# Twelve products that nothing reads, put in front of the two products of the first token unit for which TensorE waits last

## The chip, the cores and the metric

The kernel runs on one core of a Trainium2 chip. The metric is the device time of one execution in microseconds, the median of three runs. Times inside an execution come from one execution that the hardware profiler recorded; they count from the start of its span. The engines are TensorE (PE, with its weight loads PEld), VectorE (DVE), ScalarE (ACT), GpSimd (POOL) and SyncE (SP), which issues the transfers.

## What is computed

A windowed attention is followed by a gated mixing of tokens and channels. The reference, cut to what matters:

```python
# attention: q, k, v are (8, 8, 576, 64); heads 0-3 see the 32 positions up to their own,
# heads 4-7 every fourth of 128
scores = scale * np.matmul(q, k.transpose(0, 1, 3, 2))
scores = np.where(masks[None, :, :, :], scores, -1000000000.0)
scores = scores - np.max(scores, axis=-1, keepdims=True)
attn = np.exp(scores)
attn = attn / (np.sum(attn, axis=-1, keepdims=True) + 1e-09)
attn_out = np.matmul(attn, v)
# x is (8, 576, 512): the heads side by side
theta = x @ w_theta
zr = x * np.cos(theta)
zi = x * np.sin(theta)
y = einsum('ts,bsd->btd', w_tok_r, zr) + einsum('ts,bsd->btd', w_tok_i, zi)
u = x + y
return u + np.maximum(u @ w_ch, 0.0)
```

## The kernel before

The work goes batch by batch (8 batches). The attention of a batch is done in four pairs of heads: `scores` (products on TensorE into a bank of the pool s, line 468), row maxima and exponentials, `turn` (transposes on VectorE, line 525) and `pv` (products with v into the bank of tag v, line 617). For some pairs the mask is added by TensorE itself, with products of the identity (line 424) that open the score bank; then VectorE takes the row maxima from the bank (line 430) and scales them (line 438), and ScalarE reads the bank with its exponentials (line 485), five for the first part of a pair and four for the second. The bank is free when the last of them has read it. The pool s has two banks.

`theta` and `trig` make theta, sines and cosines, and `zsplit` splits each block kt of z into a rounded part zh (ScalarE, line 644, or VectorE, line 641) and the rest zl (GpSimd, line 646). There are nine blocks: 0 to 3 are x times the cosine and 4 to 7 x times the sine in four blocks of 128 tokens, and 8 holds the last 64 tokens of both.

A token unit, `token(b, d, g)`, makes one 128x288 piece of y: 128 channels d by half g of the tokens. For each block kt, in the order KORD = (0, 4, 1, 5, 2, 6, 3, 7, 8), it issues three products: zh with the upper part of the token weights (wtkh), zh with the lower part (wtkl), and zl with the upper part; 27 products in all, into one bank. `residual` then adds the bank to x on VectorE (line 825), and ScalarE and GpSimd split the sum (lines 828 and 830). Channel units, `chan`, follow in the same way (line 882). A batch has 16 units: four token units of g = 0, four of g = 1, and eight channel units. In batch 0 the units take turns on the two banks of the pool m, so that the fourth unit needs the bank whose sums the residual of the second has read.

The order on each engine is fixed ahead of time by the class `Order`, a planner with costs and ranks, for batch 0 and the beginning of batch 1, and by program order after that. In batch 0 TensorE's row is kept as the planner wrote it: the products of the first token unit stand between the last work on theta and the scores of batch 1, and each waits for its block of z. The last blocks to come are zh and zl of block 3. The second and third token unit follow directly; the scores of pairs 2 and 3 of batch 1 stand between the products of the third and fourth, and the outputs of pair 0 of batch 1 (line 617) within the fourth.

Of the kernel before, what the change touches and what calls it, by code (L numbers as in the profile page):

```python
# [10 lines left out]
BF16 = mybir.dt.bfloat16  # L11
# [7 lines left out]
DM = H * D  # L19
# [19 lines left out]
FG0 = {4: ("zl2", "zl6"), 0: ("zl3", "zl7"), 1: ("zh3", "zh7")}  # L39
COS_PSUM, SIN_PSUM = True, True  # L40
KORD = (0, 4, 1, 5, 2, 6, 3, 7, 8)
TP0 = {4: "s", 0: "s", 1: "x", 2: "t", 3: "s"}
TP = {4: "t", 0: "s", 1: "s", 2: "t", 3: "s"}

# [17 lines left out]
class Order:  # L62
# [17 lines left out]
    def signal(self, event):  # L80
        self.events[event] = self.now

    def go(self, gen, rank=None):
        if not self.live:
            for _ in gen:
                pass
            return
        self.serial += 1
        t = [self.rank if rank is None else rank, self.serial, self.now, gen, None, 0.0]
        self.tasks.append(t)  # L90
        self.advance(t)
# [60 lines left out]
def build(ctx, tc, qT, kT, vw, wth, wtk, wch, maskb, ident, identb, outT):  # L152
    nc = tc.nc
    cp = ctx.enter_context(tc.tile_pool(name="const", bufs=1))
# [15 lines left out]
    def pe(ins):  # L170
        tc.keep_in_program_order(ins)
# [13 lines left out]
    def reserve(tag):  # L185
        taken[tag] = taken.get(tag, -1) + 1
        return taken[tag]

    def take(tag, bufs, n=None):
        n = reserve(tag) if n is None else n  # L190
        if od.live:
            if n >= bufs:
                yield None, ("free", tag, n - bufs)
            if n:
                yield None, ("got", tag, n - 1)
            signal(("got", tag, n))
        return n

    def give(tag, n):
        if od.live:  # L200
            signal(("free", tag, n))

    def bank(tag, name):
        if tag == "v":
            n = yield from take(tag, 1)
            return ps_v.tile([128, 2 * DM], F32, tag=tag, name=name), (tag, n)
        pl, bufs = banks[tag]
        n = yield from take(tag, bufs)
        return pl.tile([128, DM], F32, tag=tag, name=name), (tag, n)
# [60 lines left out]
    def first_loads():  # L270
        yield "DMA", dma(3 * BW + 64)
        pin(nc.sync.dma_start(mskb, maskb.bitcast(BF16)))
        pin(nc.sync.dma_start(idb, identb.bitcast(BF16)))
        for pr in range(NP):
            yield from take(f"xh{pr}", 1, 0)
            yield from take(f"u{pr}", 1, 0)
            pqs.append(hp.tile([128, 2, S], F32R, tag=f"xh{pr}", name=f"P0_{pr}").bitcast(F32)[:, 0])
            q = hp.tile([128, 2, S], F32R, tag=f"u{pr}", name=f"q0_{pr}").bitcast(F32)
            q = q.rearrange("p a b -> p (a b)").rearrange("p (a b) -> p a b", b=2 * QB)
            k = first_k[:, KE * pr:KE * pr + KE]  # L280
            yield "DMA", dma(2 * S)
            pin(nc.sync.dma_start(q, qT[0, pr]))
            yield "DMA", dma(KE)
            pin(nc.sync.dma_start(k, kT[0, pr]))
            qks[0, pr] = (q, k, None)
            if pr == 0:
                yield "DMA", dma(128)
                pin(nc.sync.dma_start(idt, ident))
            signal(("qk", 0, pr))
        for pr in range(NP // 2):  # L290
            v = first_v[:, NJ * 128 * pr:NJ * 128 * pr + NJ * 128].rearrange("p (a b) -> p a b", b=128)
            yield "DMA", dma(NJ * 128)
            pin(nc.sync.dma_start(v, vw[0, pr]))
            for h, t in (("a", v[:, :VA]), ("b", v[:, VA:])):
                vs[h, 0, pr] = (t, None)
                signal(("v" + h, 0, pr))
        for pr in range(NP // 2, NP):
            yield from load_va(pr)
            yield from load_vb(pr)
# [354 lines left out]
    def theta0(st):  # L654
        cs = slice(128 * st, min(128 * st + 128, S))
        n = cs.stop - cs.start
        for c in range(NC):
            yield None, ("wth32", c)
            yield None, ("xe", 0, c)
            if c == 0:  # L660
                if TP0[st] == "s":
                    yield None, ("sc", 0, NP - 1)
                elif TP0[st] in "tm":
                    yield None, ("fl", 0, NP - 1)
                ths[0, st] = yield from bank(TP0[st], f"th0_{st}")
            yield "PE", 860
# [150 lines left out]
    def residual(b, d, g, ps, rel):  # L817
        ts = slice(HS * g, HS * g + HS)
        x = xf[b, d]
        if g == 0:  # L820
            yield from take(f"u{d}", 1, UH.get(d) if b == 0 else None)
            u = hp.tile([128, 2, S], F32R, tag=f"u{d}", name=f"u{b}_{d}")
            uh[b, d], ul[b, d] = u[:, 0], u[:, 1]
        yield "DVE", dve(HS)
        pin(nc.vector.tensor_tensor(x[:, ts], ps, x[:, ts], op=ALU.add))  # L825
        give(*rel)
        yield "ACT", act(HS)
        pin(nc.scalar.copy(uh[b, d][:, ts], x[:, ts]))  # L828
        yield "POOL", pool(HS)
        pin(nc.gpsimd.tensor_tensor(ul[b, d][:, ts], x[:, ts], uh[b, d][:, ts].bitcast(F32), op=ALU.subtract))  # L830
        signal(("u", b, d, g))

    def unit_bank(b, n):
        return "mmx"[n % 3] if b else "m"

    def token(b, d, g):
        yield None, ("z", b, KORD[0])
        yield None, ("wtk", g, KORD[0] // 2)
        ps, rel = yield from bank(unit_bank(b, NC * g + d), f"y{b}_{d}_{g}")
        ps = ps[:, :HS]  # L840
        cs = slice(128 * d, 128 * d + 128)
        n = 0
        for kt in KORD:
            yield None, ("z", b, kt)
            yield None, ("wtk", g, kt // 2)
            zh, zl = zs[b, kt]
            wh, wl = (w[:, HS * (kt % 2):HS * (kt % 2) + HS] for w in wtks[g, kt // 2])
            yield "PE", 369
            for l, r in ((zh, wh), (zh, wl), (zl, wh)):
                pe(nc.tensor.matmul(ps, l[:, cs], r, start=(n == 0), stop=(n == 3 * NK - 1)))  # L850
                n += 1
        signal(("tk", b, d, g))
        go(residual(b, d, g, ps, rel), RANK["evacuate"])

# [14 lines left out]
    def chan(b, e, g):  # L869
# [14 lines left out]
        go(finish(b, e, g, ps, rel), RANK["evacuate"])  # L884

    UNITS = [(token, d, g) for g in range(2) for d in range(NC)]
    UNITS += [(chan, e, g) for g in range(2) for e in range(NC)]

# [64 lines left out]
    EA, LA, LA2 = ([(t, reserve(t)) for t in ts] for ts in (EARLY, LATE, LATE2))  # L953
    XH = {p: reserve(f"xh{p}") for p in range(NP)}
    UH = {d: reserve(f"u{d}") for d in range(NC)}
    od.live = True
    go(first_loads(), 0)
    go(consts(), 0)
# [100 lines left out]
```

## Time and profile before

| | |
|---|---|
| median of 3 runs | 584.02 us (583.85 to 584.76) |
| the profiled execution | 585.12 us |
| its span | 583.3 us |
| mean granted TensorE clock | 0.987 |
| TensorE busy | 553.4 us (95%), 5464 products |
| VectorE busy | 377.9 us (65%) |
| ScalarE busy | 343.9 us (59%) |
| GpSimd busy | 222.5 us (38%) |

TensorE is busy for nearly the whole span. Its granted clock is at one of two levels, 2.4 GHz (full, 1.00 in the rows) and 1.2 GHz (half, 0.50). In a profile a product's duration contains its way through the array, so what a product costs in a row of products is read from the distance between two starts. Idle time in front of an instruction stands in brackets with the engine, the tile and the line that ended it.

### The profile page before, as it was taken

What the parts mean: (1) busy time and instruction counts of PE and PEld (TensorE: products, weight loads), DVE (VectorE), ACT (ScalarE), POOL (GpSimd) and SP (SyncE); (2) the same over time, 40 slices, a digit from 0 to 9 for tenths busy, and PEclk for the clock granted to TensorE, in tenths of its full rate; (3) what the DMA queues carried; (4) which work ended last, traced back from release to release, by engine and by line L of the source; (5) the groups of instructions that cost most, each with busy time, mean ns of one, the idle gap of its engine ahead of it and who ended that gap; (6) DMA issues with size and microseconds to landing.
All of it is one profiled execution on the core that took longest, in us unless ns stands there. A gap on an engine that the chain in (4) does not pass through costs nothing.

```text
span 583.3 us, 13997 instructions
## 1 busy us (share of the span) xinstructions
PE 553.4 (95%) x5464; PEld 503.5 (86%) x5464; DVE 377.9 (65%) x1156; ACT 343.9 (59%) x939; POOL 222.5 (38%) x206
## 2 busy tenths in 40 slices
PE   5997799999999899999999899998999899999997
PEld 3744698879999799988999799988999799989997
DVE  3779798866666768666765767666775667545112
ACT  1498967767554784459555695349645685267110
POOL 2227855525124362326324263225423262326120
PEclk9999699899999999999999999999999999999999
DMA  8990437601748056460746246470746323331002
GB/s 300 400 360 16 172 101 247 212 0 75 215 144 200 25 175 211 100 174 27 261 144 162 65 144 202 116 197 1 251 146 165 96 83 102 66 98 60 24 0 82
DMA packets 45586, 81.91 MB, mean 140 GB/s; under 512 B 3920, under 2 KB 19024, under 8 KB 45520
## 3 DMA queue, kind: packets, MB, share of 16 engines
q1 hardware_dynamic: 45520, 81.02, 43.9%
q8 instruction: 43, 0.70, 0.5%
q14 instruction: 23, 0.19, 0.1%
HBM read 64.49 MB, written 16.52 MB: 139 GB/s over the span
## 4 chain that ended last, share of the span: by engine, by line
DVE 31%; PE 29%; ACT 26%; POOL 6%; issue 4%; DMA 3%; SPq 1%; ACTq 0%; DVEq 0%
DVE pt L525 14%; PE y L850 13%; ACT P L504 10%; PE c L882 7%; PE th L685 4%; DVE P L409 4%; POOL zl L646 3%; DVE xh L599 2%; POOL P L510 2%; ACT zh L644 2%; ACT K L698 2%; ACT K L787 2%; PE s L468 2%; ACT cos L705 2%; ACT th L796 2%
## 5 line engine op out<-in xcount | busy, mean ns | idle before, releaser
L830 POOL TENSOR_TENSOR u<-x,u 128x288 fp32r<-128x288 f32 x64 | 54.9, 858 | 190.1 <-ACT u L828 190.1
L525 DVE STREAM_TRANSPOSE pt<-P 32x288 f32<-32x288 f32 x224 | 105.1, 469 | 12.1 <-POOL P L510 8.5
L882 PE MATMUL c<-u,late_wc 128*128 128x288 f32 x768 | 108.9, 295 | 0.0
L882 PEld LDWEIGHTS c<-u,late_wc 128*128 128x128 f32 x768 | 105.9, 188 | 2.8
L850 PE MATMUL y<-wtkh,zh 128*128 128x288 f32 x288 | 90.4, 314 | 1.8 <-ACT zh L644 1.8
L828 ACT CAST u<-x 128x288 fp32r<-128x288 f32 x64 | 27.4, 429 | 108.0 <-DVE x L825 108.0
L850 PE MATMUL y<-wtkh,zl 128*128 128x288 f32 x288 | 86.4, 300 | 4.0 <-POOL zl L646 4.0
L646 POOL TENSOR_TENSOR zl<-g,zh 128x512 fp32r<-128x512 f32 x40 | 52.6, 1317 | 94.8 <-ACT zh L644 81.9
L850 PE MATMUL y<-wtkl,zh 128*128 128x288 f32 x288 | 86.0, 299 | 0.0
L685 PE MATMUL th<-wthh,xh 128*128 128x512 f32 x224 | 75.1, 396 | 7.4 <-DVE g L748 7.4
L504 ACT ACTIVATE P<-P,mx 128x64 f32<-128x64 f32 x216 | 72.0, 335 | 10.3 <-DVE mx L498 9.6
L850 PE MATMUL y<-late_wt_b,zh 128*128 128x288 f32 x320 | 68.2, 297 | 0.0
L825 DVE TENSOR_TENSOR x<-y,x 128x288 f32<-128x288 f32 x64 | 28.6, 450 | 54.9 <-PE y L850 54.6
L850 PEld LDWEIGHTS y<-wtkh,zh 128*128 128x128 f32 x288 | 55.3, 192 | 5.3 <-ACT zh L644 2.9
L850 PEld LDWEIGHTS y<-wtkh,zl 128*128 128x128 f32 x288 | 55.3, 192 | 4.7 <-POOL zl L646 4.7
L685 PEld LDWEIGHTS th<-wthh,xh 128*128 128x128 f32 x224 | 42.0, 187 | 17.3 <-issue 8.4
L850 PE MATMUL y<-late_wt_a,zh 128*128 128x288 f32 x256 | 56.8, 304 | 0.0
L850 PEld LDWEIGHTS y<-wtkl,zh 128*128 128x128 f32 x288 | 55.3, 192 | 0.3 <-issue 0.3
L510 POOL TENSOR_TENSOR P<-P,sm 128x576 f32<-128x576 f32 x32 | 37.5, 1172 | 42.0 <-DVE sm L508 18.1
L850 PEld LDWEIGHTS y<-late_wt_b,zh 128*128 128x128 f32 x320 | 51.5, 189 | 0.3
L850 PE MATMUL y<-late_wt_b,zl 128*128 128x288 f32 x160 | 47.3, 296 | 0.0
L581 ACT COPY x<-o 128x576 f32<-128x576 f32 x32 | 29.7, 928 | 28.8 <-PE o L617 24.0
(108 smaller groups left out, 1107.6 us busy)
## 6 DMA issues: line engine op xcount, KB each, us to landing
q<-in_qT_dram SPq DMA_DIRECT2D x32, 576.0 KB, 5.1
va<-in_vw_dram SPq DMA_DIRECT2D x30, 320.0 KB, 3.4
k<-in_kT_dram SPq DMA_DIRECT2D x28, 304.0 KB, 5.7
out_dram<-x SPq DMA_DIRECT2D x28, 288.0 KB, 2.3
vb<-in_vw_dram SPq DMA_DIRECT2D x29, 256.0 KB, 3.8
xd<-xq SPq DMA_DIRECT2D x24, 288.0 KB, 5.2
xn<-xd SPq DMA_DIRECT2D x24, 256.0 KB, 5.1
st_wtk<-in_wtk_dram SPq DMA_DIRECT2D x8, 576.0 KB, 9.1
```

The source lines that it names most:

```text
L409: pin(nc.vector.tensor_tensor_reduce(out=P[:, n], in0=ps[:, n - g0], in1=mskb[:, mask_of(pr, n)], op0=ALU.add, op1=ALU.max, scale=1.0, sca ...
L504: table(nc.scalar.activation(P[:, n], P[:, n], AF.Exp, bias=mx[:, n:n + 1], scale=SCALE, accum_out=sm[:, n:n + 1]))
L510: pin(nc.gpsimd.tensor_tensor(P, P, sm.unsqueeze(2).to_broadcast([128, NJ, BW]), op=ALU.mult))
L525: pin(nc.vector.transpose(pmats[b, pr][k0:k0 + QB, :, hh, QB * e:QB * e + QB], P[p0:p0 + QB, :, QB * o:QB * o + QB]))
L581: pin(nc.scalar.copy(dst, src))
L646: pin(nc.gpsimd.tensor_tensor(lo, z, hi.bitcast(F32), op=ALU.subtract))
L685: pe(nc.tensor.matmul(pt, l, r, start=(n == 0), stop=(n == 3 * NC - 1)))
L825: pin(nc.vector.tensor_tensor(x[:, ts], ps, x[:, ts], op=ALU.add))
L828: pin(nc.scalar.copy(uh[b, d][:, ts], x[:, ts]))
L830: pin(nc.gpsimd.tensor_tensor(ul[b, d][:, ts], x[:, ts], uh[b, d][:, ts].bitcast(F32), op=ALU.subtract))
L850: pe(nc.tensor.matmul(ps, l[:, cs], r, start=(n == 0), stop=(n == 3 * NK - 1)))
L882: pe(nc.tensor.matmul(ps, l[:, cs], r[:, ts], start=(n == 0), stop=(n == 3 * NC - 1)))
```

## The change

Twelve products of a tile of ones with itself are put into the first token unit (batch 0, d = 0, g = 0): eight in front of the first product of block 3, and four in front of its third product. They are bf16, 128 by 512, write the bank of tag v, and nothing reads that bank before it is written anew. The bank is taken from the planner ahead of block 3 and given back at the end of the unit. The tile of ones is filled once, by VectorE, at the start of the program.

```diff
+KEEP_BUSY = {(0, 0, 0, 3, 0): 8, (0, 0, 0, 3, 2): 4}
...
             zh, zl = zs[b, kt]
             wh, wl = (w[:, HS * (kt % 2):HS * (kt % 2) + HS] for w in wtks[g, kt // 2])
+            if (b, d, g, kt) == (0, 0, 0, KORD[6]):
+                busy = yield from bank("v", "busy")
             yield "PE", 369
-            for l, r in ((zh, wh), (zh, wl), (zl, wh)):
+            for i, (l, r) in enumerate(((zh, wh), (zh, wl), (zl, wh))):
+                for _ in range(KEEP_BUSY.get((b, d, g, kt, i), 0)):
+                    pe(nc.tensor.matmul(busy[0][:, :DM], ones[:, :128], ones, start=True, stop=True))
                 pe(nc.tensor.matmul(ps, l[:, cs], r, start=(n == 0), stop=(n == 3 * NK - 1)))
                 n += 1
+        if b == d == g == 0:
+            give(*busy[1])
         signal(("tk", b, d, g))
...
+    ones = cp.tile([128, DM], BF16, name="ones")
+    nc.vector.memset(ones, 1.0)
     od.live = True
```

TensorE's row before, at the end of block 6 and in block 3 of the first unit (y_0_0 is the unit's bank; the last number of a name is a running one):

```order
L850 MATMUL y_0_0_648<-wtkl_623,zh_6_692 128x288
L850 MATMUL y_0_0_648<-wtkh_622,zl_6_693 128x288
L850 MATMUL y_0_0_648<-wtkh_526,zh_3_795 128x288
L850 MATMUL y_0_0_648<-wtkl_527,zh_3_795 128x288
L850 MATMUL y_0_0_648<-wtkh_526,zl_3_796 128x288
L850 MATMUL y_0_0_648<-wtkh_622,zh_7_754 128x288
```

The same place after the change, from the last of the eight products on:

```order
L855 LDWEIGHTS ones
L855 MATMUL busy<-ones 128x512
L856 MATMUL y_0_0_650<-wtkh_528,zh_3_797 128x288
L856 MATMUL y_0_0_650<-wtkl_529,zh_3_797 128x288
L855 LDWEIGHTS ones
L855 MATMUL busy<-ones 128x512
L855 LDWEIGHTS ones
L855 MATMUL busy<-ones 128x512
L855 LDWEIGHTS ones
L855 MATMUL busy<-ones 128x512
L855 LDWEIGHTS ones
L855 MATMUL busy<-ones 128x512
```

Eight pairs of a weight load and a product now stand between zl of block 6 and zh of block 3, and four between zh and zl of block 3; the rest of TensorE's row is as before.

VectorE's row at the start of the program, before and after:

```order
L303 MEMSET halfpi 128x1
L430 TENSOR_REDUCE mx_0_116<-s_0_0_118 128x5
```

```order
L965 MEMSET ones 128x512
L305 MEMSET halfpi 128x1
L432 TENSOR_REDUCE mx_0_118<-s_0_0_120 128x5
```

One fill is added ahead of the others; nothing else moves on VectorE, and the rows of ScalarE, GpSimd and SyncE are the same apart from line numbers.

## Rows read from the trace of the kernel before

**Rows 1.** TensorE's timeline: start us, us, engine, line, operation, tiles, idle before.

```profile
64.18 0.29 PE L850 MATMUL y<-wtkh,zl 128*128 128x288 f32 x1
66.23 0.40 PE L850 MATMUL y<-wtkh,zh 128*128 128x288 f32 x1 [1.76 <-ACT zh L644]
66.47 0.29 PE L850 MATMUL y<-wtkl,zh 128*128 128x288 f32 x1
67.87 0.61 PE L850 MATMUL y<-wtkh,zl 128*128 128x288 f32 x1 [1.11 <-POOL zl L646]
68.28 0.44 PE L850 MATMUL y<-wtkh,zh 128*128 128x288 f32 x1
...
73.80 0.30 PE L850 MATMUL y<-wtkh,zl 128*128 128x288 f32 x1
...
77.37 0.29 PE L850 MATMUL y<-wtkh,zl 128*128 128x288 f32 x1
```

**Rows 2.** Windows: stretch, length, busy time (instructions) per engine, granted clock, DMA, GB/s.

```profile
60.25:63.50 3.25, 3.25 (x41) 2.80 (x42) 2.48 (x19) 3.23 (x6) 3.25 (x4) 0.50 0.88 340
63.75:66.75 3.00, 1.24 (x8) 0.79 (x6) 3.00 (x14) 2.93 (x12) 2.02 (x3) 1.00 0.73 242
67.00:73.70 6.70, 5.83 (x24) 5.83 (x25) 4.42 (x11) 6.70 (x31) 6.07 (x6) 0.50 0.03 11
```

**Rows 3.** The chain that ended last, from 60 to 131 us: start us, us, what.

```profile
67.87 9.79 PE y L850 x52
...
83.64 3.45 DMA vb<-in_vw_dram
87.09 1.15 POOL P L510
```

**Rows 4.** TensorE's timeline around the mask products of pair 3 of batch 1.

```profile
80.77 0.40 PE L850 MATMUL y<-wtkh,zh 128*128 128x288 f32 x1
...
83.33 0.29 PE L850 MATMUL y<-wtkh,zl 128*128 128x288 f32 x1
83.55 0.31 PE L424 MATMUL s<-mskb,idb 128*128 128x64 bf16 x5
```

**Rows 5.** ScalarE's timeline: the first and the last of five exponentials.

```profile
81.91 0.31 ACT L485 ACTIVATE P<-s,mx 128x64 f32<-128x64 f32 x1 [2.35 <-DVE mx L438]
...
83.08 0.33 ACT L485 ACTIVATE P<-s,mx 128x64 f32<-128x64 f32 x1
```

**Rows 6.** VectorE's timeline from 69 to 95 us, the rows the text names.

```profile
69.20 0.17 DVE L507 TENSOR_SCALAR sm<-sm 128x9 f32<-128x9 f32 x1 [1.22 <-ACT P L504]
...
69.95 0.46 DVE L825 TENSOR_TENSOR x<-y,x 128x288 f32<-128x288 f32 x1 [0.33 <-PE y L850]
70.96 0.95 DVE L525 STREAM_TRANSPOSE pt<-P 32x288 f32<-32x288 f32 x2 [0.55 <-POOL P L510]
...
78.64 0.46 DVE L825 TENSOR_TENSOR x<-y,x 128x288 f32<-128x288 f32 x1
...
80.11 0.49 DVE L430 TENSOR_REDUCE mx<-s 128x5 f32<-128x320 f32 x1
...
81.62 0.17 DVE L438 TENSOR_SCALAR mx<-mx 128x5 f32<-128x5 f32 x1
...
85.12 0.49 DVE L430 TENSOR_REDUCE mx<-s 128x5 f32<-128x320 f32 x1 [0.86 <-PE s L468]
...
94.97 0.77 DVE L332 TENSOR_SCALAR st_wch<-st_wch 128x512 f32<-128x512 f32 x1 [0.74 <-DMA st_wch<-in_wch_dram]
```

**Rows 7.** GpSimd's timeline, the row ahead of L510 in the chain.

```profile
85.69 1.45 POOL L352 TENSOR_TENSOR late_wt_b<-st_wtk,late_wt_b 128x576 fp32r<-128x576 f32 x1 [0.77 <-ACT late_wt_b L350]
```

**Rows 8.** TensorE's timeline, two products of 512 columns at full clock.

```profile
116.68 0.40 PE L690 MATMUL th<-wthh,xh 128*128 128x512 f32 x1
116.92 0.40 PE L689 MATMUL th<-wthl,xh 128*64 128x512 f32 x1
```

**Rows 9.** VectorE's timeline, its first work behind the fills at the start.

```profile
7.79 0.49 DVE L430 TENSOR_REDUCE mx<-s 128x5 f32<-128x320 f32 x1 [6.93 <-PE s L468]
```

## The prediction, made before the changed kernel ran

> **What bounds the kernel now.** Read the stretch of the change first, in TensorE's timeline. The last product ahead of the change starts at 64.18 us. The next one, the first with zh of token block 3, starts at 66.23 after 1.76 us of idle that ScalarE's cast of zh ended; its neighbour follows at 66.47; then 1.11 us of idle end at 67.87 with GpSimd's zl [rows 1]. The granted clock was full between 63.75 and 66.75 and half from 67.0 to 73.7, although products follow one another from 67.87 on [rows 2]. So the two gaps cost twice: themselves, and a half-speed stretch behind them. The second price can be read off. From 68.28 to 73.80 there are 23 steps of 0.240 us, from 73.80 to 77.37 27 steps of 0.132 [rows 1]. At full clock the 23 would take 3.04 instead of 5.52 us: 2.48 less. The step at 67.87 (0.41 us to 68.28) would shrink to the 0.24 seen from 66.23 to 66.47: 0.17 less. Together **2.65 us**, 0.45% of the span; that is the whole stake of the change, for the gaps stay (their ends are set by ScalarE and GpSimd).
>
> Then ask whether TensorE's lead would arrive. The chain of waits says yes at first sight: it holds TensorE's products from 67.87 for 9.79 us, and runs on over the load of vb at 83.64 into GpSimd's product L510 at 87.09 [rows 3]. But look at what TensorE meets. At 83.55 it starts the mask products of scores (1,3), which overwrite a score bank; its product before started at 83.33, and a step is 0.13, so it was free at 83.46 and already stood 0.09 us [rows 4]. The bank is released by the last of five exponentials, L485, which run from 81.91 to 83.08 + 0.33 = 83.41; ScalarE had idled 2.35 us ahead of the first, waiting for VectorE's L438 [rows 5]. L438 ran at 81.62, and VectorE has no idle row between 70.96 and 85.12: transposes, the residual at 78.64, the maximum at 80.11, transposes, L438. Where does that queue begin? At 69.20 it waited 1.22 us for ScalarE's exponentials, at 69.95 0.33 us for the first token unit, at 70.96 0.55 us for GpSimd [rows 6]. ScalarE was busy for 6.70 of the 6.70 us from 67.0 to 73.7 [rows 2]. Only the 0.33 us is TensorE's, and behind it VectorE stands 0.55 us for GpSimd: an earlier residual lengthens that wait and nothing else. So in this stretch VectorE and ScalarE set the pace, and TensorE reaches the bank as it comes free.
>
> The link of the chain through vb is weak too: GpSimd was in L352 from 85.69 for 1.45 us, to 87.14, when L510 took over [rows 7]. With vb earlier L510 starts no earlier.
>
> **The change part by part.**
>
> The twelve products. No row has a bf16 product of 512 columns. The nearest below is 0.132 us (288 columns of fp32r), the nearest above the 0.24 us between the starts at 116.68 and 116.92 (512 columns) [rows 8]; I take 0.23 as the value nearest to the latter. TensorE is free at 64.18 + 0.13 = 64.31. Eight take 8 x 0.23 = 1.84 us, to 66.15; zh comes at 66.23, so they fit with 0.08 to spare; at 0.24 they end on it, at 0.132 they leave 0.87 us of the gap. Four more start at 66.47 + 0.13 = 66.60 and take 0.92, to 67.52; zl comes at 67.87: 0.35 to spare. At full clock they cost nothing, and the cover is the wait for ScalarE and for GpSimd. If zh comes late by 0.2 through them, GpSimd, which waits for ScalarE and not for TensorE, still brings zl at 67.87: nothing goes on. At half speed they would cost 0.42 each (0.23 x 0.240 / 0.132); that is weighed below.
>
> The bank. The products write the bank of the attention outputs (tag v). Its last reader was the copy of pair 3 of batch 0 and its next user is pair 0 of batch 1, whose products come behind the fourth unit; both are ordered on TensorE itself. No wait is added.
>
> The tile of ones. One fill on VectorE at the start, where it idles 6.93 us up to 7.79 [rows 9]; a fill of 512 columns costs nothing there, and at most the 0.49 us that a reduction of 320 columns takes [rows 9], which still fits. The orders of ScalarE, GpSimd and the DMA queue are the same as before.
>
> The gain, followed on. If the clock stays full, TensorE is 2.65 us ahead when the fourth unit is due: 80.77 - 2.65 = 78.12. That unit writes the bank of the second, and its residual on VectorE runs from 78.64 to 79.10 [rows 6]: TensorE stands **1.03 us**, and 1.62 us of lead is left. From 80.77 to 83.46 there are 2.69 us of its work [rows 4]; it reaches the mask products at 79.15 + 2.69 = 81.84, and the bank comes free where it did: it stands **1.66 us**. Start as before, at 83.5. 2.65 - 1.03 - 1.66 = -0.04, so within the reading of these rows nothing is left but the 0.09 us that it already stood. The loads of q, k, va and vb go out up to 2.7 us earlier, and none of them is the last that someone waits for here.
>
> Sum, against the profiled execution: 585.12 us (583.3 of span and 1.8 around it), gain 0 to 0.09. The three timed runs have their median at 584.02, 1.10 below the profiled one, so I carry the difference over: **584.0 us**.
>
> **The rivals.**
>
> A, the lead arrives (faster). It needs that VectorE's queue from 69 to 82 hangs on TensorE after all, by a wait that the trace puts down to another engine. For it: the chain's 9.79 us and its link over vb [rows 3]; the 0.33 us at 69.95. Against: no other row of VectorE from 69.2 to 82 waits for TensorE, and L352 before L510 [rows 7]. Price: the whole 2.65 gives 581.4; with the bank wait of the fourth unit kept, which is plain in the code, 1.62 gives 582.4. The Trainium skill (Perfetto Trace Analysis, Matmul Optimizations) says that TensorE's power follows its use, so products should run back to back; taken alone that promises this rival's time. The trace agrees on the clock, which fell behind the gaps [rows 2], not on what it is worth.
>
> B, the idle time is only moved (slower). The two gaps of 64 to 68 are filled, but 1.03 and 1.66 us of idle arise before 83.5, 2.69 against the 2.87 us of the two old gaps. If the clock falls behind them as it fell there, it does so where VectorE does wait for TensorE: 0.86 us at 85.12 for scores [rows 6]. Half speed costs 1 - 0.132 / 0.240 = 0.45 us per us. A stretch as long as that of 67.0 to 73.7 delays TensorE 3.0 us; VectorE then absorbs what idle it has that is not TensorE's, mainly the 0.74 us at 94.97 for a load [rows 6], with smaller ones about 1.1. Left over 1.9 us: 585.9. A stretch as short as that of 60.25 to 63.5 [rows 2] costs 1.5, less 1.1: 584.4, no change. It decides from 5.0 us of half speed, where 0.45 x 5.0 - 1.1 passes 1.17. Against it: the new gaps are apart by 2.69 us of work, the old ones by 0.4. The Trainium skill (TensorE: Matmul & The Clock Gate, the part on cycling through PSUM banks) tells of a kernel whose clock swings because TensorE idles briefly at its banks, which speaks against the change in just this place. The trace before has no such gap there, so no row decides it.
>
> C, the change doesn't do what it says: the clock falls at 66.9 all the same. Then of the four products some 2.5 run at half speed and end at about 68.1, 0.25 us late; the stretch to 73.7 stays, and TensorE reaches the bank 0.25 - 0.09 = 0.16 us late: 584.2, no change. Products that run wholly at half speed because an execution's clock is low at 64 would be worse, but then the clock before was low there too.
>
> **How the numbers follow.** A difference of 0.2%, 1.17 us, is about what a measurement of this kernel can tell from no change. The forecast has 0.56, C 0.08, B short 0.06: the same, 0.70. A has 0.18 (0.11 for 582.4, 0.07 for 581.4): faster. B long has 0.12: slower. The forecast is the likeliest, 584.0, with 583.4 to 584.8 for itself (the runs before spread from 583.85 to 584.76). The range takes in C, B short and the smaller half of A: 582.1 to 585.1, which leaves out 0.07 and 0.12.
>
> **What would show it.** In the profile of the changed kernel: twelve products of ones between 64.3 and 67.6; granted clock full from 67 to 74; 23 steps of 0.13 instead of 0.24; a new wait of about 1.0 us at the fourth unit for the residual L825 on VectorE, and one of about 1.7 us at the mask products for ScalarE's exponentials (lines count two to ten higher there); VectorE's maximum still at about 80.1, the mask products still at about 83.5. C would show half clock behind 67; B a half-clock stretch that starts near 84; A a maximum and exponentials that start earlier than 80 and 81.9. The forecast is wrong if the mask products start before 82.5 or VectorE's row at 69 to 71 moves with TensorE.

## The result and the profile after

The changed kernel takes 586.79 us (median of 22 runs, 583.86 to 589.86) against 583.93 for the kernel before (22 runs, 582.07 to 585.59): ratio 1.0044, 95% interval 1.0032 to 1.0056. It is slower by some 2.6 us (0.0044 x 584), where 584.0, no change, was forecast. The profiled execution of it was the quickest of the 22, 583.86 us with a span of 582.1; two more profiled executions (below, `a1` and `a2`) took 585.65 and 587.09. Whole spans of single executions therefore say little here, and what follows compares stretches between the same two instructions.

In the token unit the change did what was forecast. TensorE's timeline of the changed kernel (start us, us, engine, line, operation, idle before), which answers [rows 1] and [rows 4]:

```profile
60.58 0.29 PE L856 MATMUL y<-wtkh,zl 128*128 128x288 f32 x1
60.71 1.90 PE L855 MATMUL busy<-ones 128*128 128x512 bf16 x8
63.51 0.40 PE L856 MATMUL y<-wtkh,zh 128*128 128x288 f32 x1 [0.89 <-ACT zh L646]
63.75 0.29 PE L856 MATMUL y<-wtkl,zh 128*128 128x288 f32 x1
63.88 1.04 PE L855 MATMUL busy<-ones 128*128 128x512 bf16 x4
65.16 0.40 PE L856 MATMUL y<-wtkh,zl 128*128 128x288 f32 x1 [0.25 <-POOL zl L648]
65.40 0.29 PE L856 MATMUL y<-wtkh,zh 128*128 128x288 f32 x1
...
68.44 0.29 PE L856 MATMUL y<-wtkh,zl 128*128 128x288 f32 x1
...
76.43 0.40 PE L856 MATMUL y<-wtkh,zh 128*128 128x288 f32 x1 [0.95 <-DVE x L827]
...
80.82 0.31 PE L426 MATMUL s<-mskb,idb 128*128 128x64 bf16 x5 [1.54 <-ACT P L487]
```

In this execution the products of ones fit into both gaps, with 0.89 and 0.25 us to spare. The 23 steps behind the gaps, from 65.40 to 68.44, take 3.04 us instead of 5.52. Then come the two waits that were forecast, 0.95 us for the residual and 1.54 us for the exponentials. The clock column (the number ahead of the last two) is full all through, where [rows 2] show half clock:

```profile
59.00:62.00 3.00, 2.66 (x22) 1.59 (x19) 3.00 (x19) 2.97 (x6) 2.64 (x3) 1.00 0.91 304
62.00:68.00 6.00, 4.86 (x30) 3.55 (x29) 3.97 (x10) 5.95 (x33) 4.78 (x4) 1.00 0.22 84
63.50:74.00 10.50, 10.25 (x89) 9.15 (x89) 8.00 (x17) 10.50 (x40) 9.86 (x8) 1.00 0.02 6
```

The time is lost later, where the prediction did not look. Cut the span at three instructions of TensorE: the masks of scores (1,3) (83.55 before, 80.82 after), the masks of scores (2,0) (102.79 and 101.18), and the second group of L759, products that transpose x in batch 1 (126.02 and 124.83; L761 after). Behind the last one both kernels need the same time, 457.29 and 457.25 us, and so does every other kernel below (457.2 to 457.5 in all 18 profiles): whatever differs lies ahead of it. From (1,3) to (2,0) the kernel before needs 19.24 us and the changed one 20.36. TensorE's row at the masks of (2,0), before and after:

```profile
102.79 0.30 PE L424 MATMUL s<-mskb,idb 128*128 128x64 bf16 x2 [2.07 <-ACT P L485]
```

```profile
101.18 0.30 PE L426 MATMUL s<-mskb,idb 128*128 128x64 bf16 x2 [3.28 <-ACT P L487]
```

TensorE waits 1.2 us longer, for exponentials that wait for VectorE's maxima. VectorE's timeline before and after, the rows that lead there (L332 and L334 are the same operation, the first step on the loaded channel weights st_wch; L430 and L432 the maximum):

```profile
92.35 0.43 DVE L332 TENSOR_SCALAR st_wch<-st_wch 128x512 f32<-128x512 f32 x1
...
96.03 0.68 DVE L342 SCALAR_TENSOR_TENSOR st_wch<-st_wch 128x512 uint32<-128x512 uint32 x1
96.63 0.21 DVE L597 TENSOR_TENSOR xh<-x,xh 128x64 fp32r<-128x64 f32 x1
...
97.73 0.69 DVE L342 SCALAR_TENSOR_TENSOR st_wch<-st_wch 128x512 uint32<-128x512 uint32 x1
...
99.44 0.49 DVE L430 TENSOR_REDUCE mx<-s 128x5 f32<-128x320 f32 x1
```

```profile
90.44 0.43 DVE L334 TENSOR_SCALAR st_wch<-st_wch 128x512 f32<-128x512 f32 x1 [1.05 <-DMA st_wch<-in_wch_dram]
...
92.22 0.38 DVE L334 TENSOR_SCALAR st_wch<-st_wch 128x512 f32<-128x512 f32 x1
...
92.89 1.28 DVE L344 SCALAR_TENSOR_TENSOR st_wch<-st_wch 128x512 uint32<-128x512 uint32 x1
94.09 0.82 DVE L599 TENSOR_TENSOR xh<-x,xh 128x64 fp32r<-128x64 f32 x1
...
95.81 1.01 DVE L344 SCALAR_TENSOR_TENSOR st_wch<-st_wch 128x512 uint32<-128x512 uint32 x1
...
97.83 0.49 DVE L432 TENSOR_REDUCE mx<-s 128x5 f32<-128x320 f32 x1
```

Counted from the masks of (1,3), the maximum starts 15.89 us behind them before and 17.01 after: 1.12 later, which is the 1.12 us of the stretch (20.36 - 19.24). VectorE waits 1.05 us for the first st_wch; before, it hardly waited for that one, and 0.74 us for the second, which [rows 6] show at 94.97.

The wait does not reach the maximum in a straight line. The step on the second st_wch starts 11.42 us behind the masks before and 11.40 after, so up to there the new wait only replaces the old one. What comes behind it is slower: the two rows of L344 and that of L599 take 1.28, 0.82 and 1.01 us instead of 0.68, 0.21 and 0.69, 1.53 more in all. Less the 0.39 us by which the step on the second st_wch is shorter (0.38 instead of 0.77), that is 1.14, the lateness of the maximum. Beside them runs GpSimd's product L512 (L510 before), which waits for sums that VectorE makes behind the first st_wch, and so comes 0.82 us later (11.57 us behind the masks instead of 10.75). Before, it fell mostly into VectorE's wait for the second st_wch and the step behind it. GpSimd's timeline before and after:

```profile
94.30 1.15 POOL L510 TENSOR_TENSOR P<-P,sm 128x576 f32<-128x576 f32 x1 [2.07 <-DVE sm L508]
```

```profile
92.39 1.23 POOL L512 TENSOR_TENSOR P<-P,sm 128x576 f32<-128x576 f32 x1 [2.98 <-DVE sm L510]
```

The 18 profiles of this case have 72 rows of VectorE like L344 on st_wch. The 40 with no row of GpSimd beside them take 0.68 to 0.70 us, the other 32 from 0.69 to 1.29. So the lateness of the first st_wch starts the loss, and VectorE's slower rows are where it is paid. That GpSimd's work beside them makes them slower is read from these rows alone; no experiment here moves GpSimd by itself.

The load itself takes longer from issue to landing, 5.8 us instead of 4.9. The tile's view, first issue of st_wch alone, before and after:

```profile
L325 SPq DMA_DIRECT2D st_wch<-in_wch_dram x1: 432/432/432, 87.3 to 87.3; - x1
...
DMA to landing us min/median/max: 4.9/4.9/4.9
```

```profile
L327 SPq DMA_DIRECT2D st_wch<-in_wch_dram x1: 423/423/423, 84.6 to 84.6; - x1
...
DMA to landing us min/median/max: 5.8/5.8/5.8
```

It was issued 3.75 us behind the masks of (1,3) before and 3.74 after (84.56 in the chain below). So it was neither issued late nor early with respect to the work around it; something held it in the DMA engines. The chain of waits of the changed kernel runs over it:

```profile
83.53 0.64 PE s L470 x16
...
84.56 5.78 DMA st_wch<-in_wch_dram
...
90.89 0.47 DVE pt L527
```

Before, the chain ran over the second load of st_wch instead (5.21 us from its issue at 89.67).

What held it is found in the page's list of DMA queues, which has, beside the transfers of the program, queues of kind "instruction" (packets, MB, share of 16 engines):

```profile
q1 hardware_dynamic: 45520, 81.02, 43.5%
q8 instruction: 43, 0.70, 0.5%
```

43 packets of 16 KB in q8, each taking about a microsecond (0.88 to 1.85 in the trace, half of them under 0.98). TensorE executes 5476 products and as many weight loads; divided by 43 that is 255, so this is TensorE's own program being fetched; with 256 more instructions (`only_e256`, below) there are 44. The Trainium skill (Runtime: NRT & Kernel Launch, Instruction fetch mechanics) describes it: the sequencer refills its instruction memory over a DMA queue of its own in blocks of 16 KiB, 256 instructions, and the page calls the cost mostly hidden. The trace agrees on the block (0.70 MB / 43); TensorE does not wait for it here either (it is busy for 0.95 of the 0.95 us from 87.25 to 88.20), but somebody else pays.

Twenty-four more instructions (twelve products, twelve weight loads) bring the next fetch forward in the program. A load and a product take 0.132 us (3.04 / 23), so twelve pairs are worth an estimated 1.6 us of the program, and the fetch did start 6.42 us behind the masks of (1,3) instead of 8.08. The DMA view of half a microsecond around the fetch, before (91.6 to 92.1) and after (87.2 to 87.7):

```profile
q1 hardware_dynamic: 44, 0.18, 100.1%
q8 instruction: 1, 0.02, 11.6%
```

```profile
q1 hardware_dynamic: 59, 0.19, 95.3%
q8 instruction: 1, 0.02, 12.0%
...
st_wch<-in_wch_dram SPq DMA_DIRECT2D x1, 512.0 KB, 4.7
```

Both times the 16 engines were full. Before, the fetch came 4.3 us behind the issue of the first st_wch (91.63 - 87.3), when the packets of the second were under way; after, 2.7 us behind it (87.24 - 84.56), as the packets of the first began.

A packet's record names its queue and not its DMA engine, but the packets' times, read one by one, tell what happened. Packets run in sixteen lanes side by side, one for each engine, and in a lane each packet starts as the one before it ends. The load has eight packets of 4 KB in each lane, 0.16 us each, and a packet of 4 bytes that closes them. Before, all sixteen lanes close the first st_wch within 3.90 to 4.32 us of its issue, and the fetch starts behind that. After, fifteen lanes close it within 3.81 to 4.27 us, and for the next 0.79 us none does; in the sixteenth the fetch runs from 2.68 to 3.64 us in front of the load's eight packets, which close at 5.35. The count of small packets in the DMA views shows it, before (91.1 to 91.7) and after (88.3 to 88.9, then 88.9 to 89.6):

```profile
DMA packets 78, 0.27 MB, mean 444 GB/s; under 512 B 16, under 2 KB 16, under 8 KB 77
```

```profile
DMA packets 73, 0.24 MB, mean 396 GB/s; under 512 B 15, under 2 KB 15, under 8 KB 73
```

```profile
DMA packets 68, 0.28 MB, mean 398 GB/s; under 512 B 0, under 2 KB 0, under 8 KB 68
```

### The profile page after: what moved, and what is told of

Read it like the earlier page. It is cut to its first block, busy times and chain, and to the rows that moved or that the text cites. A ratio compares the mean times of both kernels' runs of the same rounds, so it can differ in the third digit from the quotient of the medians.

```text
span 582.1 us, 14022 instructions
## 1 busy us (share of the span) xinstructions
PE 549.1 (94%) x5476; PEld 498.1 (86%) x5476; DVE 379.9 (65%) x1157; ACT 344.3 (59%) x939; POOL 222.8 (38%) x206
## 4 chain that ended last, share of the span: by engine, by line
DVE 32%; PE 27%; ACT 26%; POOL 5%; DMA 5%; issue 4%; SPq 0%; ACTq 0%; DVEq 0%; POOLq 0%
DVE pt L527 16%; PE y L856 11%; ACT P L506 10%; PE c L890 7%; PE th L687 4%; DVE P L411 4%; DMA st_wtk<-in_wtk_dram 3%; POOL zl L648 3%; POOL P L512 3%; DVE xh L601 2%; ACT zh L646 2%; ACT K L700 2%; ACT K L789 2%; PE s L470 2%; ACT cos L707 2%
## 5 line engine op out<-in xcount | busy, mean ns | idle before, releaser
L830 ACT CAST u<-x 128x288 fp32r<-128x288 f32 x64 | 27.4, 429 | 108.1 <-DVE x L827 107.9
L856 PE MATMUL y<-wtkh,zh 128*128 128x288 f32 x288 | 89.2, 310 | 1.9 <-DVE x L827 1.0
L856 PEld LDWEIGHTS y<-wtkh,zh 128*128 128x128 f32 x288 | 54.1, 188 | 5.7 <-ACT zh L646 2.3
L856 PEld LDWEIGHTS y<-wtkh,zl 128*128 128x128 f32 x288 | 54.1, 188 | 4.7 <-POOL zl L648 4.7
L512 POOL TENSOR_TENSOR P<-P,sm 128x576 f32<-128x576 f32 x32 | 37.6, 1174 | 39.7 <-DVE sm L510 17.7
```

Of the source, the lines that this page charges most:

```text
L512: pin(nc.gpsimd.tensor_tensor(P, P, sm.unsqueeze(2).to_broadcast([128, NJ, BW]), op=ALU.mult))
```

## The experiments

Every kernel here has the tile of ones; ratios are to the kernel before on the same chip. The letters in the expectations name theories, each explained where it first stands.

### Two more profiled executions of the change: `a1`, `a2`

No edit.

> The changed kernel once more, unaltered: a second profiled execution. Its median over 22 runs is 586.79 us, 2.9 above the kernel before, while the execution profiled first took 583.86. H (the products meet half clock): in an execution of the usual length the clock is already at half when the eight products start; they then take about 0.43 us each, 3.4 in all instead of 1.9, and zh and zl of block 3 are used 1.5 to 2.5 us after they are ready; the row before them shows no idle time. B (the idle time is moved): the products run at full clock as in the first profile, and a half-clock stretch begins between 78 and 88 us, behind waits of about 1.0 and 1.6 us. L (the tile of ones moves the others or its fill is in the way): neither is seen, and the loss lies spread or before 60 us.

> A third profiled execution of the changed kernel, since one profile shows one course of the clock only. Expected as for the second: H half clock under the twelve products, B half clock from about 80 us on, L neither.

585.65 and 587.09 us. The masks of (1,3) stand at 81.26 and 83.51, so when this point is reached varies between executions by as much as the 2.65 us in question. In `a1` the clock was at half until 63.5 us. TensorE came to the first gap only some 1.4 us before zh was ready (2.7 in the first profile), and zh was used 0.8 us and zl 0.2 us late, less than theory H had. The wait at the masks was 1.54 us all the same, so that was swallowed too. What does not vary is the way from there to the masks of (2,0): 20.66 and 20.89 us, with waits of 3.58 and 3.80 us in front of them. VectorE's row in `a2`:

```profile
93.66 0.43 DVE L334 TENSOR_SCALAR st_wch<-st_wch 128x512 f32<-128x512 f32 x1 [1.57 <-DMA st_wch<-in_wch_dram]
```

In neither does the granted clock fall between 66 and 100 us, so rival B, which put a half-clock stretch near 84, is not what happened there.

### The tile alone: `tile_only`

```diff
-KEEP_BUSY = {(0, 0, 0, 3, 0): 8, (0, 0, 0, 3, 2): 4}
+KEEP_BUSY = {}
```

> The tile of ones, its fill and the taking of the bank stay, all twelve products are left out. L: the whole loss stays, ratio about 1.004 (586.5 us). H and B: as the kernel before, ratio 0.999 to 1.001 (583.9 us).

583.84 us, ratio 1.0011 [0.9997, 1.0024]; way 19.04 us, the wait in front of (2,0) 1.96. The tile, its fill and the taking of the bank cost nothing that can be told.

### Twelve short products: `short`

```diff
-pe(nc.tensor.matmul(busy[0][:, :DM], ones[:, :128], ones, start=True, stop=True))
+pe(nc.tensor.matmul(busy[0][:, :64], ones[:, :128], ones[:, :64], start=True, stop=True))
```

> All twelve products stay in their places, but with 64 columns each instead of 512: about 0.03 us at full clock (0.4 us in all), 0.06 at half. H: the loss goes with the columns, so an eighth of it stays: ratio 0.999 to 1.001 (584.0 us). B: the gaps are no longer filled, so no lead, no moved idle time: also about 1.000. L: ratio about 1.004. If the loss comes from the mere presence of the products (the switch of weights, a wait), it stays at 1.003 to 1.005.

586.29 us, ratio 1.0046 [1.0033, 1.006]: the whole loss with products of an eighth of the width. Columns are not what costs, and theory H, by which long products meet a half clock, falls as the cause.

### Holding the loads of (2,0): `hold`

```diff
+        if n == 2 * NP:
+            yield None, "held"
...
+        if (b, key[2], g0) == (1, 2, 0):
+            pin(nc.vector.tensor_copy(scratch, qks[b, 2][0][:, 0, :1]))
+            signal("held")
...
```

> The changed kernel with one fill-in on VectorE: right behind the row maximum of scores (1,2) it copies one column of that pair's q, so that the loads of q and k for (2,0), and va and vb behind them in SyncE's order, cannot go out before about 80.6 us although TensorE's lead stays. D (the lead sends these loads out 2 to 3 us early, the transfer engines fall idle before the next burst, and the first st_wch lands about 1 us later than before): the first st_wch lands 5 us after its issue again, VectorE waits under 0.3 us for it, the stall of TensorE at about 100 us is about 2 us, and the ratio falls from 1.0044 to 0.999 to 1.0015. S (the lead or the products cost by themselves, whatever the loads do): ratio 1.003 to 1.005 as the changed kernel.

587.79 us, ratio 1.0068 [1.0047, 1.0089]: worse, so an early issue of the loads (theory D) is not the cause. Theory S, as it was put, had 1.005 at most. Holding q and k moved the first st_wch too, to 86.6 us, 5.2 behind the masks of (1,3). It stays in the DMA engines about as long as in the changed kernel (6.2 us against 5.8 to 6.3), and the wait for it grew:

```profile
93.34 0.43 DVE L336 TENSOR_SCALAR st_wch<-st_wch 128x512 f32<-128x512 f32 x1 [1.89 <-DMA st_wch<-in_wch_dram]
```

### The lead given back: `giveback`

```diff
-KEEP_BUSY = {(0, 0, 0, 3, 0): 8, (0, 0, 0, 3, 2): 4}
+KEEP_BUSY = {(0, 0, 0, 3, 0): 8, (0, 0, 0, 3, 2): 4, (0, 1, 0, 0, 0): 11}
...
```

The lines left out keep the bank until the end of the second unit.

> The changed kernel with eleven more products of ones at the head of the second token unit, 2.6 us at full clock: TensorE's lead is spent before the scores (1,2) whose end releases the loads. D: loads at the old time, so no loss: ratio 0.999 to 1.0015, the stall at about 100 us about 2 us. S, as a cost of the products themselves: no better than the changed kernel, ratio 1.004 or more; as a cost of the lead: as D.

586.55 us, ratio 1.0044 [1.0028, 1.006], way 20.59 us. TensorE reaches the masks of (1,3) without any wait in this profile, so the lead is gone and the loss is not. D falls here as well.

### Only eight, only four: `eight`, `four`

```diff
-KEEP_BUSY = {(0, 0, 0, 3, 0): 8, (0, 0, 0, 3, 2): 4}
+KEEP_BUSY = {(0, 0, 0, 3, 0): 8}
```

> Only the eight products in front of zh of block 3; the four in front of zl are left out. If the loss follows the clock being kept (the lead), and eight are enough for it, ratio 1.003 to 1.005; if the four are needed, 0.999 to 1.0015. S, as a cost of each product: two thirds of the loss, ratio 1.003.

> Only the four products in front of zl of block 3. If the clock is kept by them alone, ratio 1.003 to 1.005; else 0.999 to 1.0015. S, as a cost of each product: a third of the loss, ratio 1.0015.

583.73 us, ratio 0.9996 [0.9978, 1.0014], and 584.13, 0.9999 [0.998, 1.0018]; the way is 19.05 us in both. `eight` has the two waits of the forecast (0.94 and 1.54 us) and loses nothing: a lead of TensorE is swallowed, as the prediction said, and harmless. Twelve cost 2.6 us and eight none, so it is not a price per product either (theory S). What was left was something that depends on the count and not on the width: TensorE's program itself.

### The instructions without the gaps: `early24`, `look_e24`, `early16`

```diff
-KEEP_BUSY = {(0, 0, 0, 3, 0): 8, (0, 0, 0, 3, 2): 4}
+KEEP_BUSY = {}
+AHEAD = 12
...
+    for _ in range(AHEAD):
+        pe(nc.tensor.matmul(ahead[:128, :64], ones[:, :128], ones[:, :64], start=True, stop=True))
```

The products stand at the very start of TensorE's row, where it waits for the first loads; `early16` has eight of them. With an empty table the bank is not taken in the token unit.

> The kernel before, with the tile of ones and twelve products of 64 columns (24 instructions with their weight loads) at the very start of TensorE's row, where it waits for the first loads; no product of ones in the token unit. Theory F (the 24 instructions bring the fetch of TensorE's next 16 KB of instructions forward, ahead of the packets of the first load st_wch on one of the DMA engines, and that load lands about 1 us later): the loss of the changed kernel appears without any product in the gaps: ratio 1.003 to 1.005, the fetch about 6.6 us behind the mask products of scores (1,3) instead of 8.1, the first st_wch 5.8 to 6.3 us from issue to landing instead of 4.9, TensorE's wait ahead of the masks of scores (2,0) 3.2 us or more instead of 2.1. Theory P (the products in the gaps do it, by the lead or the clock): ratio 1.000 +- 0.0015, first st_wch 4.9 us, that wait 2.1 us.

> The same with eight products, 16 instructions, the number that lost nothing in the gap. Theory F: the fetch comes between those of the two other cases, still behind the packets of the first st_wch: ratio 1.000 +- 0.0015, first st_wch 4.6 to 5.1 us. If the loss follows smoothly from the number of instructions, ratio about 1.003. Theory P: 1.000.

> A second look at the kernel with 24 instructions at the start and no product in the gaps. Theory F: the way from the masks of (1,3) to those of (2,0) is again 20.4 to 20.9 us, with the fetch 6.4 to 6.8 us behind the former and the first st_wch 5.8 us or more from issue to landing.

`early24`: 586.87 us, ratio 1.0058 [1.004, 1.0076], without one product in the gaps. The landing of its first st_wch (tile's view), VectorE's wait for it and TensorE's wait (the two timelines):

```profile
DMA to landing us min/median/max: 6.2/6.2/6.2
```

```profile
92.69 0.43 DVE L335 TENSOR_SCALAR st_wch<-st_wch 128x512 f32<-128x512 f32 x1 [1.48 <-DMA st_wch<-in_wch_dram]
```

```profile
103.43 0.42 PE L427 MATMUL s<-mskb,idb 128*128 128x64 bf16 x2 [3.71 <-ACT P L488]
```

The same loss through the same rows, 80 us and more behind any product of ones. The second profiled execution (`look_e24`) has a way of 20.45 us and a landing of 5.9. `early16` has neither (way 19.17, landing 4.9, wait 2.08); its ratio is 1.0015 [1.0001, 1.0028].

### The fetch moved out of the burst, and back to its place: `after_e60`, `after_e232`, `look_e232`

The changed kernel with 30 products of 64 columns, or 116 of 16 columns, at the start; 24 + 232 is one whole block.

```diff
 KEEP_BUSY = {(0, 0, 0, 3, 0): 8, (0, 0, 0, 3, 2): 4}
+AHEAD = 30
...
```

> The changed kernel with 30 further products of 64 columns (60 instructions) at the very start of TensorE's row. Theory F: the fetch comes some 84 instructions earlier than before, about 3 us behind the masks of (1,3), ahead of the issue of the first st_wch: that load lands in 4.6 to 5.1 us, and the loss is gone: ratio 0.998 to 1.001. Theory P: the twelve products are still there, ratio 1.004.

> The changed kernel with 116 products of 16 columns (232 instructions) at the very start of TensorE's row; with the 24 of the change that makes 256, a whole fetch, so that the fetches behind the token unit stand at the same instructions as before. Theory F: fetch again about 8 us behind the masks of (1,3), first st_wch 4.6 to 5.1 us, ratio 0.999 to 1.0015, unless the 116 products delay the first scores by more than those scores wait for loads. Theory P: ratio 1.004 or more.

> A second look at the changed kernel with 116 products at the start. If its remaining 0.3% lies ahead of the masks of (1,3), these start later than the 80.8 to 83.8 us of the other kernels, and the way from them to the masks of (2,0) is 19.0 to 19.3 us; if it lies behind, that way is 20.4 or more in this execution.

`after_e60`: 583.7 us, ratio 0.9998 [0.9981, 1.0015]. All twelve products are in the gaps, the forecast's waits are there (0.94 and 1.54 us), and the loss is gone. The fetch falls into a pause of the loads; the DMA view from 86.15 to 86.65 us shows nothing else but it:

```profile
q8 instruction: 1, 0.02, 12.0%
```

The first st_wch lands after 4.6 us, VectorE has no wait for either (its later rows are the slow ones, 1.28, 0.82 and 0.99 us, and the way is no shorter than in `eight`), and TensorE's wait ahead of the masks of (2,0) is short again:

```profile
91.87 0.43 DVE L335 TENSOR_SCALAR st_wch<-st_wch 128x512 f32<-128x512 f32 x1
...
93.66 0.38 DVE L335 TENSOR_SCALAR st_wch<-st_wch 128x512 f32<-128x512 f32 x1
```

```profile
102.58 0.30 PE L427 MATMUL s<-mskb,idb 128*128 128x64 bf16 x2 [2.23 <-ACT P L488]
```

`after_e232` puts the fetch back to 7.98 us behind the masks, and in both of its profiles the stretch is as before: way 19.06 and 19.05 us, landing 4.7, the wait in front of (2,0) 1.96. Its time did not follow: 585.72 us, ratio 1.0033 [1.0017, 1.0048], which is outside the range of theory F (0.999 to 1.0015) and only a little under that of theory P (1.004). Theory F had made one exception, that the 116 products delay the first scores; the next two runs are about that.

### What the products at the start cost: `only_e256`, `only_e60`

No product in the gaps; 128 products of 16 columns, or 30 of 64, at the start (AHEAD = 128 and 30).

> The kernel before with 128 products of 16 columns (256 instructions, one whole fetch) at the start of TensorE's row and no product in the gaps; every later fetch stands at the same instruction as before. If the products at the start cost time by themselves: ratio 1.002 to 1.004, as with the 116. If they are free and the twelve products in the gaps cost 0.3%: ratio 1.000 +- 0.0015. First st_wch 4.6 to 5.1 us either way.

> The kernel before with 30 products of 64 columns (60 instructions) at the start and none in the gaps. Theory F: the fetch comes about 4 to 5.5 us behind the masks of (1,3), in front of or inside the packets of the first st_wch; ahead of them (under 4) no loss, ratio 0.998 to 1.001; among the first of them a loss of up to 0.4%. The wait ahead of the masks of (2,0) follows the landing of st_wch: 2.1 us with 5 us, 3.2 or more with 5.8 or more.

`only_e256`, a whole block: 585.39 us, ratio 1.0019 [1.0005, 1.0033], with the way at 19.07 us and the landing at 4.8. So a long row of products at the start costs some 1 us by itself, ahead of the masks of (1,3) or in executions that the profile did not catch (the masks stand at 82.36 and 84.38 in the two profiles of `after_e232`, at 82.68 here, within the spread of the others); with `after_e232` that leaves 0.8 us (1.0033 - 1.0019), less than the two intervals allow to tell from nothing. Where that microsecond lies isn't settled. `only_e60` has the fetch 0.6 us behind the issue of the first st_wch, as its burst begins, and a part of the loss: 585.69 us, ratio 1.0027 [1.0011, 1.0043].

```profile
93.38 0.43 DVE L335 TENSOR_SCALAR st_wch<-st_wch 128x512 f32<-128x512 f32 x1 [0.76 <-DMA st_wch<-in_wch_dram]
```

```profile
104.11 0.30 PE L427 MATMUL s<-mskb,idb 128*128 128x64 bf16 x2 [2.97 <-ACT P L488]
```

### All profiles side by side

The start of the fetch counts from the issue of the first st_wch; "way" is from the masks of (1,3) to those of (2,0), "second way" from there to the second group of L759 (named L761 or so in the others). All in us.

| kernel | fetch | first st_wch lands after | way | second way | ratio |
|---|---|---|---|---|---|
| after_e60 | -0.8 | 4.6 | 19.31 | 23.66 | 0.9998 |
| only_e60 | 0.6 | 5.5 | 20.07 | 23.67 | 1.0027 |
| the change | 2.7 | 5.8 | 20.36 | 23.65 | 1.0044 |
| short | 2.8 | 5.9 | 20.56 | 24.72 | 1.0046 |
| look_e24 | 2.8 | 5.9 | 20.45 | 24.00 | (one run) |
| giveback | 2.9 | 6.0 | 20.59 | 24.70 | 1.0044 |
| a1 | 3.0 | 6.1 | 20.66 | 24.70 | (one run) |
| a2 | 3.0 | 6.3 | 20.89 | 23.68 | (one run) |
| early24 | 3.0 | 6.2 | 20.79 | 24.32 | 1.0058 |
| hold | 3.0 | 6.2 | 22.68 | 24.63 | 1.0068 |
| four | 4.0 | 4.7 | 19.05 | 24.09 | 0.9999 |
| only_e256 | 4.0 | 4.8 | 19.07 | 24.21 | 1.0019 |
| eight | 4.1 | 4.6 | 19.05 | 24.18 | 0.9996 |
| early16 | 4.1 | 4.9 | 19.17 | 24.08 | 1.0015 |
| tile_only | 4.1 | 4.6 | 19.04 | 23.42 | 1.0011 |
| after_e232 | 4.2 | 4.7 | 19.06 | 24.06 | 1.0033 |
| look_e232 | 4.2 | 4.7 | 19.05 | 24.30 | (one run) |
| before | 4.3 | 4.9 | 19.24 | 23.23 | 1 |

Eighteen profiles fall into two groups with nothing between: where the fetch starts 0.6 to 3.0 us behind the issue of the first st_wch, that load takes 5.5 us or more and the way 20.07 us or more; where it starts ahead of it or 4.0 us and more behind it, 4.9 at most and 19.31 at most. The first column decides the landing and the way, wherever the extra instructions stand; the ratio follows except in `after_e232` and `only_e256`.

The second way is longest, 24.32 to 24.72, in `short`, `giveback`, `a1`, `early24` and `hold`. In these five the granted clock falls during TensorE's wait of 3.3 to 4.1 us ahead of the masks of (2,0) and stays at half for 6.8 us (in `a1` from 101.1 to 107.9). In the other thirteen the half-clock stretch there lasts 3.4 us or there is none.

## Why the prediction was wrong

**The gaps, right.** Twelve products fit into them (in `a1`, at half clock, with 0.8 and 0.2 us over). In the first profile, eight were to take 1.84 us and took from 60.71 to at most 62.62; zh came 0.89 us later. The clock stayed full, and the 23 steps took 3.04 us, as worked out.

**The lead swallowed, right.** Waits of 1.03 and 1.66 us were forecast, 0.95 and 1.54 came, and `eight`, `four` and `after_e60` confirm in measured time that a lead brings nothing: 0.9996, 0.9999 and 0.9998. Rival A falls with them, and so does any hope in the 2.65 us of the stake. One sign that the prediction set against itself did appear, and means nothing: the masks of (1,3) start before 82.5 in two of the three profiles of the change (80.82 and 81.26), but they do so in `tile_only` (80.93), which has none of the products.

**"At full clock they cost nothing", the step that failed.** The cover named was the wait for ScalarE and GpSimd, and that cover held. But the prediction costed the products only as time on TensorE. They are also 24 instructions in TensorE's program, and a program is data that somebody has to load. In the sum this term was 0; it measured 1.50 us in the way: the mean of seven profiles with the fetch at 2.7 to 3.0 (the change, short, look_e24, giveback, a1, a2, early24; `hold`, which has an edit of its own, left out) is 20.61, that of the nine without a late landing (after_e60 and the rows from 4.0 on) 19.12, some 1.5 less. The second way adds 0.34 (24.25 against 23.91, the same groups), though it scatters by 1.1 us within each group. Together 1.84, against 2.6 by the median and 1.9 by the low end of the interval. Since the time behind the second way is the same everywhere, the rest lies ahead of the masks of (1,3) or in executions that no profile caught; it is open.

**"None of them is the last that someone waits for", the second step that failed.** It was said of q, k, va and vb, and no run here speaks against that. But [rows 6] held the warning: the 0.74 us at 94.97 is VectorE waiting for a load in a stretch in which the DMA engines are full. In rival B the prediction used that row as slack that would absorb a delay. It did absorb one: the step on the second st_wch starts 11.42 us behind the masks of (1,3) before and 11.40 after. What it did not count is that VectorE's later rows then ran beside GpSimd's and took 1.53 us more. In the nine profiles with a late landing VectorE has no wait from the first st_wch to the maximum and needs 7.4 us for it, so that every further tenth of lateness reaches the masks of (2,0).

**Rival B, right in sign and near in size, by luck: not its mechanism.** It gave 585.9 for a half-clock stretch near 84 us. None of the three profiles of the changed kernel has one: the new idle time of 1.54 us at the masks of (1,3) left the clock where it was. Only `hold` has one, at half clock from 82.75 to 86.0, and it is the slowest of all (1.0068). Yet half speed behind moved idle time does play a part, 20 us later: of the seven late profiles above, the four with 6.8 us of half clock around the masks of (2,0) have a second way of 24.61 on average, the three with 3.4 us 23.78. So the 0.34 us of the second way go with the clock, which fell in a wait that the late load had made longer.

What is shown is that it matters where the fetch falls among the loads, by taking the products out of the gaps and keeping the instructions (`early24`) and by keeping the products and adding instructions (`after_e60`). That the fetch and the late packets of st_wch met on one DMA engine is read from the packets' times, since no record names the engine. The size agrees: a load spread over 16 engines is as late as the latest of them, and that lane closed 1.08 us behind the fifteenth (5.35 - 4.27), with a packet of 0.96 us in front.

The Trainium skill (DMA: Bandwidth & Descriptors, Queues, rings and completion order) has each engine take turns between queues, a whole packet at a time. The trace agrees, if what a load puts on one engine (nine packets of the profile) is taken for one packet of the page: in 15 of the 16 profiles in which the engines were full, the fetch starts within 4 ns of the end of a 4-byte packet, where a load's lane closes.

That also fits the steps in which the fetch moves. The lanes of two loads that follow one another close some 1.25 us apart (2.65 to 3.07 and 3.90 to 4.32 us before), and among full engines the fetch starts at 2.7 to 3.0 us or 4.0 to 4.3, never between. Sixteen instructions leave it where it was (7.86 us behind the masks in `eight` against 7.89 in `tile_only`), 24 move it by 1.3 to 1.7, about one such turn. When TensorE asked for the block the trace does not show, so this stays an argument.

## What to carry to other kernels

Work that is hidden on its engine still lengthens that engine's program, and the program is fetched through the same DMA engines as the data: where a kernel has a stretch with full DMA engines and a load on which someone waits, look in the list of DMA queues for the instruction packets and at when they start. A short delay can also grow behind the wait that it causes: compare the length of the rows on either side of it, not only the waits. A difference of some tenths of a per cent that appears with any edit of the instruction count, whatever the instructions do, is best tested by moving the same number of them to a place where the engine idles. And filling the idle time of an engine that waits for others later on brought nothing here, although 23 products took 3.04 us instead of 5.52.

## What the runs showed of the hardware

- TensorE's instructions came in 43 packets of 16 KB in this kernel, each 0.88 to 1.85 us on a DMA engine. Where one of them started 0.6 to 3.0 us behind the issue of a load (st_wch), the load took 5.5 to 6.3 us to land instead of 4.6 to 4.9; in the profile read packet by packet it stood 0.96 us in front of the load's packets in one of sixteen lanes.
- A row of VectorE on 128x512 elements (L344) took 0.68 to 0.70 us with no row of GpSimd beside it and up to 1.29 with one; a row on 128x64 (L599) 0.21 and 0.82.
- The granted clock's course differs from one execution of a kernel to the next: in `a1` it was at half from 56.75 to 63.5 us, in the first profile of the same kernel not before 102.5. It stayed full over the token unit in `eight` too, with the second gap open. One profile doesn't show what holds it.
- The point at which the masks of (1,3) start differs by 2.7 us between executions of one kernel (80.82, 81.26 and 83.51 for the change), which is as much as the whole stake; only stretches behind a common instruction could be compared. It goes with the speed of the first products: 20 score products take 1.34 us as late as 13.76 us in the profile of the kernel before (masks at 83.55), but 1.04 at 9.89 and 0.80 at 12.82 in that of the change (80.82).
